# A fused attention and two-layer MLP kernel: the low-part subtraction of a weight tile moved ahead of the next tile's sign step, and the first tiles' conversion rearranged

## The chip, the cores and the metric

The kernel runs on one core of a Trainium2 chip. The metric is the device time of one execution in microseconds (us); lower is better. A profile of one execution gives the time of every instruction on the engines: TensorE (PE in the rows, PEld for its weight loads), VectorE (DVE), ScalarE (ACT), GpSimd (POOL), and SyncE (SP), which issues most DMA transfers.

## The reference

Three stages follow each other. Attention runs in chunks of 64 positions; its output, as a 2304 x 512 matrix x, goes through an MLP with a SiLU, and that result through a gated MLP.

```python
scores = scale * np.matmul(q_c, k_c.transpose(0, 1, 2, 4, 3))   # chunks of 64, 32 heads in all
attn = softmax(scores)
x = np.matmul(attn, v_c)                # as 2304 x 512
h = x @ w_in                            # 512 x 2048
y = (h / (1 + np.exp(-h))) @ w_out      # 2048 x 512
out = ((y @ w_a) * (y @ w_b)) @ w_out2  # 512 x 1536 twice, 1536 x 512
```

The weights arrive as 64-bit floating-point numbers. The kernel turns them into 32-bit ones itself, and splits each into a high part and a low part, since every product is made as three matmuls (high x high, high x low, low x high).

## The kernel before, in words

**Blocks and steps.** The 2304 tokens are 18 tiles of 128. Block 0 is tiles 0 to 3, the side block (`SIDE`) is tiles 4 and 5, and three more blocks of four tiles follow. A step k of the first MLP takes one block and one m of 16 slices of 128 of its hidden width. `front_a` makes the hidden slice (12 matmuls of 512 columns, line L370) and its SiLU on ScalarE: `g` at L399 and its high part `ghi` at L400; `finish` subtracts on VectorE to get the low part `glo` (L396). `back_a` multiplies by the slice of w_out into four accumulating banks (L418). During block 0's 16 steps the side block's fronts and backs, 256 columns wide, go along. In these steps the order on TensorE is: front(k+1), side back(k), side front(k+1), back(k).

**Conversion of a weight tile.** The 32 tiles of w_in and w_out, two for each m, are converted while block 0 runs. A tile passes these functions:

- `fetch`: SyncE loads it into one of three buffers `raws` (L130).
- `scaled`: ScalarE copies the upper words with a scale (L147).
- `magnitude`: two VectorE instructions (L155, L158).
- `begin`: two VectorE instructions that set the sign and the low bits (L174, L178); with the last one the raw buffer is free for the third fetch after it.
- `upper`: ScalarE copies the rounded high part into the tile `wA` (L196).
- `lower`: VectorE subtracts it from the value, which gives the low part (L203). It reads what `upper` wrote, so it waits for it.

`weights` is one call of this pipeline: it fetches a tile, and takes three earlier tiles a stage further. `prep_a` calls it twice in a step, after the SiLU of front(k+1) and after that of side front(k+1). Within a call the order on ScalarE is `upper`, `scaled`; on VectorE it is `magnitude`, `begin`, `lower`. `magnitude` and `begin` work on a later tile than `lower` does. Each engine takes its instructions in the order in which the code issues them (`tc.manual_schedule()`).

**The beginning.** Attention of tiles 0 to 5, the first conversions and the first front and back are written out by hand, as a list of calls: `S(i)` makes scores, `Tr(i, bank)` the transposes (L312) and `rest["P", i]()` their copy out by ScalarE (L316); `V(i, bank)` makes the output of the attention (64x64 matmuls, L335), `rest["X", i]()` its high part on ScalarE (L347), and `rest["L", i]()` its low part on VectorE (L351). `busy(n)` issues n matmuls on a tile of zeros (L705), whose result nobody reads; each shows as two records. They go to the PSUM bank with the tag "sA". The PSUM pool holds one buffer for each tag, so a new tile in bank "sA" waits for the last read of the tile that was in it. `V(4, "sA")` uses this bank too.

The part of the hand-written list around the change, before:

```python
V(4, "sA")
rest["X", 4]()
pend[0], silu = front_a(main[0], 0, "mm", gpool, True)
upper()
Tr(5, "at")
rest["L", 4]()
lower()
silu()
rest["P", 5]()
scaled()
busy(2)
V(5, "mm")
finish(pend, 0)
```

`magnitude`, `begin`, `busy(2)` and `back(0)` follow, then the high and low parts of tile 5, two calls of `prep_a`, and `side_front(0)`. The tile called the third below is the w_in slice of m = 1; it is the one whose `scaled`, `magnitude` and `begin` stand here.

Of the kernel before, what the change touches and what calls it, by code (L numbers as in the profile page):

```python
# [22 lines left out]
def chunk_attention_silu_mlp_gated_mlp(  # L23
# [79 lines left out]
    def bank(tag, shape):  # L103
        return psum.tile(shape, F32, tag=tag, name="ps_" + tag)

    def slot(name, dt=F32R):
        return big.tile([P, 4 * DM], dt, tag="b", name=name)
# [19 lines left out]
    def fetch(src, dest):  # L127
        raw = raws[:, turn[0] % RAWS]
        turn[0] += 1
        nc.sync.dma_start(out=raw, in_=src)  # L130
        fetched.append((dest, raw))

    def leave(n=0):

        while len(leaving) > n:
            dst, src = leaving.pop(0)
            nc.sync.dma_start(out=dst, in_=src)

    def words(raw):
        w32 = raw.bitcast(U32).rearrange("p (f t) -> p f t", t=2)  # L140
        return w32[:, :, 0], w32[:, :, 1]

    def scaled():

        dest, raw = fetched.pop(0)
        w = spool.tile([P, DM], F32, tag="tmp", name="w", bufs=3)
        nc.scalar.activation(w, words(raw)[1].bitcast(F32), AF.Copy, scale=2.0**111)  # L147
        opened.append((dest, raw, w))

    def magnitude():  # L150

        if not opened:
            return
        w = opened[0][2]
        nc.vector.tensor_scalar(  # L155
            out=w, in0=w, scalar1=2.0**-126, scalar2=2.0**-97, op0=ALU.mult, op1=ALU.mult
        )
        nc.vector.tensor_scalar(  # L158
            out=w.bitcast(U32),
            in0=w.bitcast(U32),  # L160
            scalar1=3,
            scalar2=0x7FFFFFFF,
            op0=ALU.logical_shift_left,
            op1=ALU.bitwise_and,
        )

    def begin():

        if not opened:
            return  # L170
        dest, raw, w = opened.pop(0)
        low, high = words(raw)
        wu = w.bitcast(U32)
        nc.vector.scalar_tensor_tensor(  # L174
            out=wu, in0=high, scalar=0x80000000, in1=wu,
            op0=ALU.bitwise_and, op1=ALU.bitwise_or,
        )
        nc.vector.scalar_tensor_tensor(  # L178
            out=wu, in0=low, scalar=29, in1=wu,
            op0=ALU.logical_shift_right, op1=ALU.bitwise_or,  # L180
        )
        if dest[0] == "f":
            wf[dest[1:]] = d = dram.tile([P, DM], F32, name=f"wf{dest[1]}{dest[2]}")
            leaving.append((d, w))
        else:
            stage_1.append((dest, w))

    def upper():
        if not stage_1:
            return  # L190
        dest, w = stage_1.pop()
        _, m, j = dest
        if m not in slots_a:
            slots_a[m] = slot("wA").rearrange("p (j n) -> p j n", j=4)
        hl = slots_a[m][:, 2 * j:2 * j + 2]
        nc.scalar.activation(hl[:, 0], w, AF.Copy)  # L196
        stage_2.append((dest, hl, w))

    def lower():
        if not stage_2:  # L200
            return
        dest, hl, w = stage_2.pop()
        nc.vector.tensor_tensor(out=hl[:, 1], in0=w, in1=hl[:, 0].bitcast(F32), op=ALU.subtract)  # L203
        wA.setdefault(dest[1], {})[dest[2]] = hl[:, 0], hl[:, 1]

    def weights(src, dest):

        leave()
        fetch(src, dest)
        upper()  # L210
        magnitude()
        begin()
        lower()
        scaled()


# [91 lines left out]
    def att_transpose(i, ptag, where, later=False):  # L308
        s = soft.pop(i).rearrange("p h g k -> p h (g k)")
        ps = bank(ptag, [P, KT, P])  # L310
        for hp in range(KT):
            nc.tensor.transpose(ps[:, hp, :], s[:, hp, :], ident)  # L312
        prob[i] = att_tile(where, "pt", i).rearrange("p (h n) -> p h n", h=KT)

        def evacuate():
            nc.scalar.activation(prob[i], ps, AF.Copy)  # L316

        if later:
            return evacuate
        evacuate()  # L320

    def att_values(i, ptags, x, o, later=False, beside=None):
        w = P // len(ptags)
        if beside is None:
            banks = [bank(t, [P, KT, w]) for t in ptags]
        else:
            banks = [t[:, 1 - r] for r, t in enumerate(soft[beside])]
        va = vs.pop(i).rearrange("p (a h d) -> p a h d", a=2, h=KT)
        half = [slice(0, 64), slice(64, 128)]
        for hp in range(KT):  # L330
            for a in range(2):
                for r in range(2):

                    ps, part, n = (banks[0], r, half[a]) if len(banks) == 1 else (banks[r], a, half[0])
                    nc.tensor.matmul(  # L335
                        ps[half[part], hp, n],
                        lhsT=va[half[r], a, hp, :],
                        rhs=prob[i][half[r], hp, half[a]],
                        start=True,
                        stop=True,  # L340
                    )
        parts = [[a[:, :, o + w * j:o + w * j + w] for a in x] for j in range(len(banks))]
        del prob[i]

        def upper():
            for ps, (hi, _) in zip(banks, parts):
                nc.scalar.activation(hi, ps, AF.Copy)  # L347

        def lower():
            for ps, (hi, lo) in zip(banks, parts):  # L350
                nc.vector.tensor_tensor(out=lo, in0=ps, in1=hi.bitcast(F32), op=ALU.subtract)  # L351

        if later:
            return upper, lower
        upper()
        lower()
# [21 lines left out]
    def front_a(b, m, ptag, pool, later=False):  # L378
        n = width(b)
        ps = bank(ptag, [P, n])  # L380
        product(ps, wA[m][0], x_t[b])
        ghi = pool.tile([P, n], F32R, tag="ghi", name="ghi")
        glo = pool.tile([P, n], F32R, tag="glo", name="glo")
        if b == SIDE:
            g = side.tile([P, n], F32, tag="g", name="g")
        elif "g" in late:
            g = late["g"].tile([P, n], F32, tag="g", name="g", bufs=2)
        elif "b" in late:
            g = spool.tile([P, n], F32, tag="tmp", name="g", bufs=3)
        else:  # L390
            if "g1" not in late:
                late["g1"] = late["att"].tile([P, DM], F32, tag="at", name="g")
            g = late["g1"]

        def finish():
            nc.vector.tensor_tensor(out=glo, in0=g, in1=ghi.bitcast(F32), op=ALU.subtract)  # L396

        def silu():
            nc.scalar.activation(g, ps, AF.Silu)  # L399
            nc.scalar.activation(ghi, ps, AF.Silu)  # L400

        if later:
            return (ghi, glo, finish), silu
        silu()
        return ghi, glo, finish
# [239 lines left out]
    def next_a():  # L645
        m, j = units_a[done[0]]
        done[0] += 1
        return (w_in, w_out)[j][m], ("a", m, j)
# [33 lines left out]
    with tc.manual_schedule():  # L682
# [18 lines left out]
        def busy(n):  # L701

            ps = bank("sA", [P, P])
            for _ in range(n):
                nc.tensor.matmul(ps, lhsT=zero, rhs=zero, start=True, stop=True)  # L705

        def half(i):
            if blocks[0][1] > i:
                return x_t[0], i * P
            return x_t[SIDE], (i - blocks[0][1]) * P  # L710
# [9 lines left out]
        def v_in(*tiles):  # L720
            for i in tiles:
                load_v(i, W, nc.sync)
# [12 lines left out]
        qk_in(5)  # L735
        v_in(4)
        v_in(5)


        side_bank = {-1: "at", 0: "at", 1: "at"}  # L740

# [45 lines left out]
        def back(k):  # L787
            b, m = steps[k]
            back_a(b, m, pend.pop(k))
# [9 lines left out]
        def finish(g, k):  # L799
            if k in g:  # L800
                g[k][2]()
# [3 lines left out]
        rest = {}  # L805
# [4 lines left out]
        def Tr(i, tag):  # L810
            rest["P", i] = att_transpose(i, tag, W, later=True)

        def V(i, tag):
            rest["X", i], rest["L", i] = att_values(i, (tag,), *half(i), later=True)
# [35 lines left out]
        rest["X", 1]()  # L850
        att_max(4, W, True)
        begin()
        fetch(*next_a())
        Tr(3, "sA")
        rest["P", 3]()
        rest["L", 1]()
# [22 lines left out]
        rest["X", 4]()  # L879
        pend[0], silu = front_a(main[0], 0, "mm", gpool, True)  # L880
        upper()
        Tr(5, "at")
        rest["L", 4]()
        lower()
        silu()
        rest["P", 5]()
        scaled()
        busy(2)
        V(5, "mm")
        finish(pend, 0)  # L890
        magnitude()
        begin()
        busy(2)
        back(0)
        rest["X", 5]()
# [430 lines left out]
```

## Time and profile before

| | us |
|---|---|
| median of 3 runs | 863.20 (862.88 to 863.54) |
| the profiled execution | 862.69 |
| its span, first to last instruction | 860.9 |
| TensorE busy in the span | 846.5 (98%) |
| VectorE busy | 566.7 (66%) |
| ScalarE busy | 398.5 (46%) |

The span is 1.8 us shorter than the time of the same execution. The mean granted clock of TensorE was 0.999 of full speed. Busy shares are averages over stages with different limits; of the 14.4 us in which TensorE was idle, 3.6 lie behind its last matmul and most of the rest in the first 46 us.

### The profile page before, as it was taken

To read this page: it belongs to the slowest core of one execution; us is meant where nothing else is said; L and a number is where in the kernel's file an instruction comes from. 1 tells how busy PE (TensorE), PEld (TensorE's weight loads), DVE (VectorE), ACT (ScalarE), POOL (GpSimd) and SP (SyncE) were. 2 spreads that over 40 slices of the span, in tenths; PEclk is the share of its full clock that TensorE was granted. 3 is DMA by queue.
4 is the path that set the end of the run, shared out by engine and by line. 5 is a ranking of instruction groups with operands and counts; after the bars stand their busy time and mean duration, and the time that the engine had idled before them with its cause. 6 is when DMAs were issued, how large, how long until landed. Compare 5 with 4: busy or idle time off the path is not lost.

```text
span 860.9 us, 14124 instructions
## 1 busy us (share of the span) xinstructions
PE 846.5 (98%) x5474; PEld 769.5 (89%) x5474; DVE 566.7 (66%) x1029; ACT 398.5 (46%) x769; POOL 50.2 (6%) x91
## 2 busy tenths in 40 slices
PE   7999999999999999999999999999999999999998
PEld 7788888888888888888889999999999999999998
DVE  6886877855567755757865997584454594454563
ACT  5645546535454455434545554463333373333252
POOL 0000000010010100023201110000000000000000
PEclk9999999999999999999999999999999999999999
DMA  8354353337455654467799887878666888666761
GB/s 294 100 174 132 123 161 121 100 118 238 147 174 172 217 165 169 152 226 269 265 343 372 314 296 309 306 297 294 256 249 254 306 313 265 245 252 252 288 226 56
DMA packets 54034, 193.85 MB, mean 225 GB/s; under 512 B 5904, under 2 KB 13584, under 8 KB 45520
## 3 DMA queue, kind: packets, MB, share of 16 engines
q1 hardware_dynamic: 46752, 169.76, 55.5%
q0 software_dynamic: 6928, 22.81, 8.0%
q8 instruction: 43, 0.70, 0.3%
q10 hardware_dynamic: 288, 0.39, 0.1%
q14 instruction: 23, 0.19, 0.1%
HBM read 141.03 MB, written 51.90 MB: 224 GB/s over the span
## 4 chain that ended last, share of the span: by engine, by line
PE 86%; issue 5%; ACT 3%; DMA 3%; DVE 3%; POOL 0%; POOLq 0%; ACTq 0%; DVEq 0%
PE ps_acc L972 19%; PE ps_acc L418 19%; PE ps_mm L370 15%; PE ps_sA L370 7%; PE ps_at L972 5%; PE ps_sA L972 5%; PE ps_sB L972 4%; PE ps_mm L972 4%; DMA raws<-wf 2%; PE ps_sA L418 1%; PE ps_sB L418 1%; PE ps_at L370 1%; PE ps_at L253 1%; PE ps_at L335 1%; PE ps_sA L705 1%
## 5 line engine op out<-in xcount | busy, mean ns | idle before, releaser
L972 PE MATMUL ps_acc<-xo,ring 128*128 128x384 f32 x868 | 168.2, 334 | 0.6 <-DVE gq L1047 0.6
L418 PE MATMUL ps_acc<-ghi,wA 128*128 128x512 f32 x512 | 159.2, 392 | 0.0
L972 PEld LDWEIGHTS ps_acc<-xo,ring 128*128 128x128 f32 x868 | 152.1, 188 | 1.1 <-DVE gq L1047 1.1
L418 PEld LDWEIGHTS ps_acc<-ghi,wA 128*128 128x128 f32 x512 | 94.2, 188 | 19.1
L370 PE MATMUL ps_mm<-xhi,wA 128*128 128x512 f32 (+1 forms) x400 | 101.3, 375 | 3.2 <-ACT wA L196 3.2
L418 PE MATMUL ps_acc<-glo,wA 128*128 128x512 f32 x256 | 99.9, 390 | 0.0
L370 PEld LDWEIGHTS ps_mm<-xhi,wA 128*128 128x128 f32 x400 | 70.2, 188 | 17.3 <-ACT wA L196 5.1
L399 ACT ACTIVATE g<-ps_mm 128x512 f32<-128x512 f32 (+1 forms) x50 | 28.0, 559 | 102.5 <-PE ps_mm L370 96.3
L396 DVE TENSOR_TENSOR glo<-g,ghi 128x512 fp32r<-128x512 f32 x80 | 50.7, 633 | 27.2 <-ACT ghi L400 27.0
L418 PEld LDWEIGHTS ps_acc<-glo,wA 128*128 128x128 f32 x256 | 48.1, 188 | 10.2
L1107 DVE TENSOR_TENSOR u<-gq,u 128x384 fp32r<-128x384 f32 x84 | 44.5, 553 | 17.4 <-ACT u L1106 16.9
L1106 ACT ACTIVATE u<-gq 128x384 fp32r<-128x384 f32 x84 | 40.6, 516 | 30.5 <-DVE gq L1047 28.6
L972 PE MATMUL ps_acc<-u,ring 128*128 128x384 f32 x272 | 53.6, 337 | 0.3
L147 ACT ACTIVATE w<-raws 128x512 f32<-128x512 f32 x68 | 45.5, 670 | 16.6 <-DMA raws<-w_b 8.8
L370 PE MATMUL ps_mm<-xlo,wA 128*128 128x512 f32 (+1 forms) x200 | 49.9, 371 | 0.6 <-DVE xlo L351 0.6
L370 PE MATMUL ps_sA<-xhi,wA 128*128 128x512 f32 x184 | 49.6, 391 | 0.0
L972 PEld LDWEIGHTS ps_acc<-u,ring 128*128 128x128 f32 x272 | 47.6, 188 | 1.3 <-ACT gq L981 0.9
L178 DVE SCALAR_TENSOR_TENSOR w<-raws,w 128x512 uint32<-128x512 uint32 x68 | 47.1, 692 | 2.3
L174 DVE SCALAR_TENSOR_TENSOR w<-raws,w 128x512 uint32<-128x512 uint32 x68 | 47.1, 692 | 2.3
L972 PE MATMUL ps_at<-xo,ring 128*128 128x384 f32 x231 | 47.8, 334 | 0.0
L972 PE MATMUL ps_sB<-xo,ring 128*128 128x384 f32 x220 | 44.9, 334 | 0.0
L972 PE MATMUL ps_sA<-xo,ring 128*128 128x384 f32 x213 | 44.4, 335 | 0.1
(183 smaller groups left out, 1413.5 us busy)
## 6 DMA issues: line engine op xcount, KB each, us to landing
ring<-w SPq DMA_DIRECT2D x30, 1024.0 KB, 7.3
ring<-wg SPq DMA_DIRECT2D x24, 1024.0 KB, 5.1
ring<-wg SPq DMA_DIRECT2D x24, 768.0 KB, 6.3
wg<-ring SPq DMA_DIRECT2D x12, 1024.0 KB, 6.6
wf<-w SPq DMA_DIRECT2D x36, 256.0 KB, 2.2
wg<-ring SPq DMA_DIRECT2D x12, 768.0 KB, 6.5
raws<-w_in SPq DMA_DIRECT2D x16, 512.0 KB, 3.5
raws<-w_out SPq DMA_DIRECT2D x16, 512.0 KB, 3.5
```

The source lines that it names most:

```text
L147: nc.scalar.activation(w, words(raw)[1].bitcast(F32), AF.Copy, scale=2.0**111)
L174: nc.vector.scalar_tensor_tensor(out=wu, in0=high, scalar=0x80000000, in1=wu, op0=ALU.bitwise_and, op1=ALU.bitwise_or,)
L178: nc.vector.scalar_tensor_tensor(out=wu, in0=low, scalar=29, in1=wu, op0=ALU.logical_shift_right, op1=ALU.bitwise_or,)
L253: nc.tensor.matmul(soft[i][j % len(soft[i])][n, j, hp, :], lhsT=q[r, hp, n], rhs=k[r, hp, n], start=True, stop=True,)
L335: nc.tensor.matmul(ps[half[part], hp, n], lhsT=va[half[r], a, hp, :], rhs=prob[i][half[r], hp, half[a]], start=True, stop=True,)
L370: nc.tensor.matmul(ps, lhsT=a[:, kk * P:(kk + 1) * P], rhs=b[:, kk, :], start=(j == 0 and kk == 0), stop=(j == 2 and kk == KT - 1),)
L396: nc.vector.tensor_tensor(out=glo, in0=g, in1=ghi.bitcast(F32), op=ALU.subtract)
L399: nc.scalar.activation(g, ps, AF.Silu)
L418: nc.tensor.matmul(acc_t[b][j], lhsT=a[:, j * P:(j + 1) * P], rhs=g, start=(m == 0 and i == 0 and (b != SIDE or j % 2 == 0)), stop=(m == M ...
L972: nc.tensor.matmul(ps, lhsT=a, rhs=b, start=first and i == 0, stop=last and i == 2, skip_group_check=True,)
L1106: nc.scalar.activation(hi, src, AF.Copy)
L1107: nc.vector.tensor_tensor(out=lo, in0=src, in1=hi.bitcast(F32), op=ALU.subtract)
```

## The change

There are two parts. In `weights`, `lower` is issued ahead of `begin`. In the hand-written beginning, the third fetch is issued right after the attention's loads, `scaled` of the third tile goes ahead of `Tr(5)`, `magnitude` ahead of `finish`, and `rest["L", 4]()`, the low part of tile 4 of x, goes from before the SiLU to behind `begin`.

```diff
@@ weights
         upper()
         magnitude()
+        lower()
         begin()
-        lower()
         scaled()
@@ beginning
         v_in(5)
-
+        fetch(*next_a())
...
         begin()
-        fetch(*next_a())
         Tr(3, "sA")
...
         upper()
+        scaled()
         Tr(5, "at")
-        rest["L", 4]()
         lower()
         silu()
         rest["P", 5]()
-        scaled()
         busy(2)
         V(5, "mm")
+        magnitude()
         finish(pend, 0)
-        magnitude()
         begin()
+        rest["L", 4]()
         busy(2)
         back(0)
```

VectorE at the beginning, from the end of tile 5's softmax (L303) to the low part of tile 5 of x (the second L351). In the kernel before:

```order
L303 TENSOR_TENSOR start<-start,rs 128x2x4x64
L351 TENSOR_TENSOR xlo<-ps_sA,xhi 128x4x128
L203 TENSOR_TENSOR wA<-w,wA 128x512
L396 TENSOR_TENSOR glo<-g,ghi 128x512
L155 TENSOR_SCALAR w<-w 128x512
L158 TENSOR_SCALAR w<-w 128x512
L174 SCALAR_TENSOR_TENSOR w<-raws,w 128x512
L178 SCALAR_TENSOR_TENSOR w<-raws,w 128x512
L351 TENSOR_TENSOR xlo<-ps_mm,xhi 128x4x128
```

The same place in the changed kernel:

```order
L303 TENSOR_TENSOR start<-start,rs 128x2x4x64
L203 TENSOR_TENSOR wA<-w,wA 128x512
L155 TENSOR_SCALAR w<-w 128x512
L158 TENSOR_SCALAR w<-w 128x512
L396 TENSOR_TENSOR glo<-g,ghi 128x512
L174 SCALAR_TENSOR_TENSOR w<-raws,w 128x512
L178 SCALAR_TENSOR_TENSOR w<-raws,w 128x512
L351 TENSOR_TENSOR xlo<-ps_sA,xhi 128x4x128
L351 TENSOR_TENSOR xlo<-ps_mm,xhi 128x4x128
```

The read of bank "sA" (L351 on ps_sA) went from the first place behind the softmax to the seventh, behind the subtraction for `glo` and both instructions of `begin`. TensorE's own order is the same in both kernels: the transposes of tile 5, two busy matmuls into ps_sA, the 64x64 matmuls of V(5), two more busy matmuls, back(0).

VectorE in the first call of step 0, from `glo` of side front(0) to `glo` of front(1). In the kernel before:

```order
L396 TENSOR_TENSOR glo<-g,ghi 128x256
L155 TENSOR_SCALAR w<-w 128x512
L158 TENSOR_SCALAR w<-w 128x512
L174 SCALAR_TENSOR_TENSOR w<-raws,w 128x512
L178 SCALAR_TENSOR_TENSOR w<-raws,w 128x512
L203 TENSOR_TENSOR wA<-w,wA 128x512
L396 TENSOR_TENSOR glo<-g,ghi 128x512
```

In the changed kernel:

```order
L396 TENSOR_TENSOR glo<-g,ghi 128x256
L155 TENSOR_SCALAR w<-w 128x512
L158 TENSOR_SCALAR w<-w 128x512
L203 TENSOR_TENSOR wA<-w,wA 128x512
L174 SCALAR_TENSOR_TENSOR w<-raws,w 128x512
L178 SCALAR_TENSOR_TENSOR w<-raws,w 128x512
L396 TENSOR_TENSOR glo<-g,ghi 128x512
```

The subtraction of the earlier tile, L203, now stands ahead of L174 and L178 of the next one, and so in each later call. On SyncE the order of the transfers is the same in both kernels; the third fetch stood directly behind the attention's loads already.

## Rows read from the trace of the kernel before

**Rows 1.** The page: engines' busy time, and the chain that ended last by engine.
```profile
PE 846.5 (98%) x5474; PEld 769.5 (89%) x5474; DVE 566.7 (66%) x1029; ACT 398.5 (46%) x769; POOL 50.2 (6%) x91
...
PE 86%; issue 5%; ACT 3%; DMA 3%; DVE 3%; POOL 0%; POOLq 0%; ACTq 0%; DVEq 0%
```

**Rows 2.** Waits of TensorE: us in total, times, longest.
```profile
PE ps_mm L370 <- ACT wA L196: 3.2, 5, 1.3
```

**Rows 3.** Timeline of TensorE: start, us, instruction, count, [idle before, its releaser].
```profile
30.96 0.60 PE L312 MATMUL ps_at<-ident,start 128*128 128x128 f32 x4
31.40 0.69 PE L705 MATMUL ps_sA<-start 128*128 128x128 f32 x4
32.79 1.15 PE L335 MATMUL ps_mm<-start 64*64 64x64 f32 x32 [0.70 <-ACT start L316]
33.87 0.71 PE L705 MATMUL ps_sA<-start 128*128 128x128 f32 x4
34.33 0.71 PE L418 MATMUL ps_acc<-ghi,wA 128*128 128x512 f32 x2
```

**Rows 4.** Timeline of VectorE, 30 to 36 us.
```profile
30.02 0.69 DVE L303 TENSOR_TENSOR start<-start,rs 128x512 f32<-128x512 f32 x1
30.64 0.68 DVE L351 TENSOR_TENSOR xlo<-ps_sA,xhi 128x512 fp32r<-128x512 f32 x1
31.24 0.68 DVE L203 TENSOR_TENSOR wA<-w,wA 128x512 fp32r<-128x512 f32 x1
32.28 0.69 DVE L396 TENSOR_TENSOR glo<-g,ghi 128x512 fp32r<-128x512 f32 x1 [0.36 <-ACT ghi L400]
33.32 0.43 DVE L155 TENSOR_SCALAR w<-w 128x512 f32<-128x512 f32 x1 [0.35 <-ACT w L147]
...
34.25 0.69 DVE L174 SCALAR_TENSOR_TENSOR w<-raws,w 128x512 uint32<-128x512 uint32 x1
34.97 0.69 DVE L178 SCALAR_TENSOR_TENSOR w<-raws,w 128x512 uint32<-128x512 uint32 x1
35.58 0.68 DVE L351 TENSOR_TENSOR xlo<-ps_mm,xhi 128x512 fp32r<-128x512 f32 x1
```

**Rows 5.** Timeline of ScalarE, 27 to 34 us.
```profile
27.89 0.63 ACT L196 ACTIVATE wA<-w 128x512 fp32r<-128x512 f32 x1
...
31.16 0.60 ACT L399 ACTIVATE g<-ps_mm 128x512 f32<-128x512 f32 x1 [1.34 <-PE ps_mm L370]
...
32.61 0.68 ACT L147 ACTIVATE w<-raws 128x512 f32<-128x512 f32 x1
```

**Rows 6.** Timelines of VectorE, ScalarE and TensorE at step 0.
```profile
43.27 0.69 DVE L203 TENSOR_TENSOR wA<-w,wA 128x512 fp32r<-128x512 f32 x1 [1.09 <-ACT wA L196]
...
44.99 0.63 ACT L196 ACTIVATE wA<-w 128x512 fp32r<-128x512 f32 x1
...
45.68 1.20 PE L370 MATMUL ps_mm<-xhi,wA 128*128 128x512 f32 x4 [1.27 <-ACT wA L196]
```

**Rows 7.** Timelines of VectorE and ScalarE in a later step, with attention of tile 6.
```profile
67.86 0.69 DVE L203 TENSOR_TENSOR wA<-w,wA 128x512 fp32r<-128x512 f32 x1 [2.40 <-ACT wA L196]
...
69.19 0.69 DVE L272 TENSOR_TENSOR s<-ps_at,mx 128x512 f32<-128x512 f32 x1
...
71.87 0.63 ACT L283 ACTIVATE s<-s 128x512 f32<-128x512 f32 x1
```

**Rows 8.** Timeline of TensorE: its first matmuls, its longest early pause, its last matmuls.
```profile
1.09 5.37 PE L705 MATMUL ps_sA<-start 128*128 128x128 f32 x24 [1.09 <-DVE start L699]
...
10.04 0.81 PE L253 MATMUL ps_acc<-start 64*64 64x64 f32 x32 [1.62 <-DMA start<-kt]
...
856.12 1.21 PE L972 MATMUL ps_sA<-u,ring 128*128 128x384 f32 x6
```

**Rows 9.** Stretches at the end: us, busy by engine, granted clock, DMA share, GB/s.
```profile
859.00:859.50 0.50, 0.00 (x0) 0.00 (x0) 0.00 (x0) 0.00 (x0) 0.00 (x0) 1.00 0.57 203
859.50:860.00 0.50, 0.00 (x0) 0.00 (x0) 0.00 (x0) 0.00 (x0) 0.00 (x0) 0.54 0.00 0
```

## The prediction, made before the result

> **What bounds the kernel now.** I read the page first: TensorE is busy for 846.5 of 860.9 us, and 86% of the chain that ended last is on it [rows 1]. So a change counts where it makes TensorE wait longer or shorter, and nowhere else. The waits of TensorE come next. Those for converted weight tiles (matmul L370 for ScalarE's copy L196) are five, 3.2 us in all, the longest 1.3 [rows 2]; this is all that a better order of the conversion could win. None of the waits names the subtraction L203. Then the timelines of the beginning, engine by engine, since there the change rewrites the order [rows 3, 4, 5], and two places in the steps behind it [rows 6, 7].
>
> The reader is to see one thing in the beginning. TensorE issues two busy matmuls into bank ps_sA at 31.40 [rows 3], and VectorE's read L351 of that bank, the low part of tile 4, started at 30.64 and took 0.68, so it ended at 31.32 [rows 4]. The busy matmuls came 0.08 us behind it. The view of waits shows no idle time there, because the transposes before (30.96, for 0.60) filled it. The dependence is there all the same: one buffer for each tag, and a new tile in it must wait for the last read of the old one.
>
> **The change, part by part.**
>
> *The read of ps_sA.* In the changed order L351 stands behind L203, L155, L158, L396, L174 and L178. TensorE's order is not changed, so the busy matmuls still wait for L351, and V(5) and back(0) stand behind them. With the slots of VectorE (from one start to the next) I place the new row:
> - L203 takes the slot that L351 had, at 30.64, and the next one starts 0.60 later, at 31.24.
> - `magnitude` (L155 and L158) takes 34.25 - 33.32 = 0.93, to 32.17. Its input is there, see below.
> - L396 still waits for `ghi`, which comes from ScalarE behind front(0); so it starts at 32.28 as before. Its slot is 0.60, as that of L351: 32.88.
> - L174 takes 34.97 - 34.25 = 0.72, to 33.60; L178 takes 35.58 - 34.97 = 0.61, to 34.21 [rows 4].
> - L351 runs from 34.21 to 34.89, instead of to 31.32.
>
> With the same 0.08 the busy matmuls start at 34.97. Four records of them hold TensorE for 34.33 - 33.87 = 0.46, so V(5) starts at 35.43 instead of 32.79, 2.64 later [rows 3]. The 0.70 of idle time that stood ahead of V(5), for ScalarE's copy L316, is used up in this. The rest of the beginning hangs on V(5) in order (busy, back(0) at 34.33, the side block), so it is all late by **2.64**. TensorE has no slack to give it back: what it waits for later, it waits for relative to its own products.
>
> *The steps: L203 ahead of L174.* L203 waits for `upper`, which ScalarE does behind the SiLU of the same call. So far this wait cost nothing, as L174 and L178 ran ahead of it. Now they wait too, and the next tile's `upper` waits for them. At step 0 this reaches TensorE. L203 starts at 43.27, when its copy is done [rows 6]. In the new order L174 starts 0.60 later at 43.87, L178 at 44.59, and that ends at 45.28. ScalarE's next L196 started at 44.99, and TensorE's front waits for exactly that one (1.27, at 45.68) [rows 6]. It is late by 45.28 - 44.99 = **0.29**.
>
> In the later steps the delay is covered. The hardest is a step with attention, where L203 waited 2.40 us and started at 67.86 [rows 7]. L174 and L178 now push the attention's subtraction L272 back by 0.72 + 0.61 = 1.33: it ends at 69.19 + 0.69 + 1.33 = 71.21, and the exponential that reads it starts at 71.87 [rows 7], behind a table load that does not wait for it. So 0.66 is left. If that cover were gone, each of the four such steps could lose up to 1.33, 5.3 in all; I take nothing, and keep it for the upper end. There is no gain either: TensorE waits for L196, not for L203.
>
> *Moved earlier.* `scaled` (0.68) now stands behind L196, which ends at 28.52; ScalarE was idle for 1.34 ahead of the SiLU at 31.16, waiting for TensorE [rows 5]. It fits in, and `magnitude` finds it done at 31.24. The fetch keeps its place on SyncE. The tile's `begin` ends at 34.3 instead of 35.66, but its copy L196 stands on ScalarE behind the high part of tile 5, which now follows the late V(5). So of this head start nothing is left, and nothing waited for it. All these I cost at nothing; without their cover `scaled` would cost its 0.68.
>
> *The clock.* TensorE's pause grows: its transposes end at 31.56, the next matmul comes at 34.97, so 3.4 us. A pause of 1.62 us, ahead of 10.04, left the granted clock at 1.00 [rows 8]. At the end of the kernel the last matmuls ended at 856.12 + 1.21 = 857.33, and the clock fell to half (0.5, that is 1.2 of 2.4 GHz) in the stretch from 859.50 on, 2.2 us after them [rows 8, 9]. The new pause is longer than that. So I expect the clock to fall in it or right behind it. What a fall costs no row shows in the middle of the kernel. The bound below is nothing: the clock stays or comes back at once. For the bound above I take the start: busy matmuls ran there for 5.37 us at 5.37 / 24 = 0.22 us a record, against 0.46 / 4 = 0.115 later [rows 3, 8], so half speed for some 5.2 us; half of that is 2.6 lost. I take **1.8**, nearer to the upper end, since the row of the start is the only one with a price.
>
> The Trainium skill (TensorE: Matmul & The Clock Gate, "Why this matters for your kernels") warns of such idle gaps between bursts of matmuls, after which the clock is back at half until the engine has been busy again. By this rule the sum has the clock's term; without it it ends at 2.9. The end of this trace agrees with it, at 2.2 us.
>
> **The sum.** 2.64 + 0.29 = 2.93 of waiting, and 1.8 for the clock: 4.7. Against the profiled execution's own time, 860.9 + 1.8 outside the span = 862.7, this gives 867.4. The median of the runs is 0.5 above that execution, so 863.2 + 4.7 = 867.9, and I say **868.0 us**.
>
> **Rivals.**
> - *The clock stays up.* Then 863.2 + 2.93 = 866.1. For it: no pause inside the kernel was followed by a lower clock. Against: none was half as long.
> - *The delay is given back.* If VectorE and ScalarE, being ahead of a late TensorE, had the tiles ready, the 3.2 us of waits for L196 would vanish: 863.2 + 2.93 - 3.2 = 862.9, no change. Against: the copies stand on ScalarE behind the SiLU of TensorE's own product, and so move along with it.
> - *Faster.* The place is the same wait, L370 for L196. If the busy matmuls did not hang on L351 and the earlier `lower` let the copies come sooner, all 3.2 us could go: 860.0. It decides in its favour only if the busy matmuls stay at about 31.4, and the wait at 45.68 shrinks. The 0.08 between L351's end and the busy matmuls speaks against it.
> - *The steps lose as well.* If the 0.66 ahead of the exponential is not there (a later start of L203, a late transfer), up to 5.3 more: 868 to 873, I take 871.
>
> The Trainium skill (PSUM — Partial Sum Buffer, "Engine vs sequencer instructions") says that matmuls start and complete in program order. By this V(5) cannot pass the waiting busy matmuls; if it could, it would start at 32.79 and the 2.64 would not be. The matmuls' starts in the trace agree: they stand in program order, 31.40, 32.79, 33.87, 34.33 [rows 3].
>
> **How the numbers follow.** The clock falls: 0.50. It stays: 0.35. The steps lose as well: 0.07. Given back: 0.05. Faster: 0.03. A change under 0.2% (1.7 us) can't be told from none here. Both likely cases are slower by more than that, so slower 0.92, same 0.05, faster 0.03. For the range: if the clock stays, 866.1, and 0.5 less if VectorE's slots are a little shorter; if it falls, up to 866.1 + 2.6 = 868.7, and an engine that runs slow right behind its pause may lose 1 more. That makes 865.6 to 869.8, which leaves out the last three cases and little more.
>
> **What would show it.** The busy matmuls L705 start near 35.0, with some 3.4 us idle ahead of them, put down to VectorE's L351 on ps_sA; V(5) near 35.4. The wait ahead of step 0's second front, 1.27 before, is near 1.6. The four waits of about 0.5 us later stay. The granted clock is below 1.00 for some us from about 34 on; if it is 1.00 throughout, the term of 1.8 is wrong. If the busy matmuls start at 31.4, the prediction is wrong altogether.

## The result, and the profile after

The changed kernel took 867.32 us (median of 6 runs, 866.87 to 869.22), the kernel before on the same chip 862.90. The ratio is 1.0054, with a 95% interval from 1.0041 to 1.0067: slower by 3.5 to 5.8 us. The span of the profiled execution grew from 860.9 to 865.9 us.

The new wait stands in the view of TensorE's waits of the changed kernel (us in total, times, longest):

```profile
PE ps_mm L370 <- ACT wA L196: 3.5, 5, 1.6
PE ps_sA L705 <- DVE xlo L351: 3.4, 1, 3.4
```

The first line answers to [rows 2]; the second had no counterpart. The timeline of TensorE at the beginning, for [rows 3]:

```profile
31.44 0.60 PE L312 MATMUL ps_at<-ident,start 128*128 128x128 f32 x4
35.44 0.71 PE L705 MATMUL ps_sA<-start 128*128 128x128 f32 x4 [3.40 <-DVE xlo L351]
36.08 1.46 PE L335 MATMUL ps_mm<-start 64*64 64x64 f32 x32
37.47 1.22 PE L705 MATMUL ps_sA<-start 128*128 128x128 f32 x4
38.34 1.20 PE L418 MATMUL ps_acc<-ghi,wA 128*128 128x512 f32 x2
...
43.47 1.08 PE L370 MATMUL ps_mm<-xhi,wA 128*128 128x512 f32 x4
```

The timeline of VectorE there, for [rows 4], shows what the busy matmuls (L705) waited for. The read of ps_sA starts at 34.70, behind six other instructions, and ends at 35.38:

```profile
31.10 0.69 DVE L203 TENSOR_TENSOR wA<-w,wA 128x512 fp32r<-128x512 f32 x1
31.70 0.42 DVE L155 TENSOR_SCALAR w<-w 128x512 f32<-128x512 f32 x1
...
32.76 0.69 DVE L396 TENSOR_TENSOR glo<-g,ghi 128x512 fp32r<-128x512 f32 x1 [0.17 <-ACT ghi L400]
33.37 0.69 DVE L174 SCALAR_TENSOR_TENSOR w<-raws,w 128x512 uint32<-128x512 uint32 x1
34.09 0.69 DVE L178 SCALAR_TENSOR_TENSOR w<-raws,w 128x512 uint32<-128x512 uint32 x1
34.70 0.68 DVE L351 TENSOR_TENSOR xlo<-ps_sA,xhi 128x512 fp32r<-128x512 f32 x1
```

Behind the pause the granted clock fell to half. In these stretches of the changed kernel the first number after the POOL column is the granted clock:

```profile
36.00:37.00 1.00, 1.00 (x28) 0.92 (x28) 0.00 (x0) 0.00 (x0) 0.00 (x0) 0.86 0.72 242
37.00:38.00 1.00, 1.00 (x13) 0.88 (x11) 0.00 (x0) 0.42 (x1) 0.00 (x0) 0.50 0.59 238
...
39.00:40.00 1.00, 1.00 (x4) 0.81 (x3) 0.97 (x3) 0.85 (x2) 0.00 (x0) 0.50 0.00 0
40.00:41.00 1.00, 1.00 (x5) 0.78 (x5) 0.97 (x2) 0.00 (x0) 0.00 (x0) 0.93 0.00 0
```

From the shares 0.86 and 0.93 it was at half from about 36.7 to 40.1 us. At step 0, for [rows 6], the timelines of VectorE, ScalarE and TensorE:

```profile
48.09 0.69 DVE L203 TENSOR_TENSOR wA<-w,wA 128x512 fp32r<-128x512 f32 x1 [2.51 <-ACT wA L196]
...
49.42 0.69 DVE L178 SCALAR_TENSOR_TENSOR w<-raws,w 128x512 uint32<-128x512 uint32 x1
...
50.15 0.63 ACT L196 ACTIVATE wA<-w 128x512 fp32r<-128x512 f32 x1 [0.21 <-DVE w L178]
...
50.83 1.20 PE L370 MATMUL ps_mm<-xhi,wA 128*128 128x512 f32 x4 [1.59 <-ACT wA L196]
```

ScalarE's copy L196 now waits for `begin` (L178), and TensorE's wait for that copy is 1.59 us instead of 1.27. In the step with attention, for [rows 7], the subtraction L272 moved close to the exponential, but not past it:

```profile
75.68 0.69 DVE L272 TENSOR_TENSOR s<-ps_at,mx 128x512 f32<-128x512 f32 x1
...
77.04 0.64 ACT L283 ACTIVATE s<-s 128x512 f32<-128x512 f32 x1
```

It ends at 76.37, and 0.67 is left. The four later waits of TensorE for L196 stayed at 0.47 to 0.48.

**Where the 5.0 us of the span went.** From the transposes of tile 5 to V(5) there are 36.08 - 31.44 = 4.64 us, before 32.79 - 30.96 = 1.83 [rows 3]: 2.81 more. From V(5) to the first front of the steps there are 43.47 - 36.08 = 7.39 us; in the kernel before that front stood here in TensorE's timeline:

```profile
38.61 1.09 PE L370 MATMUL ps_mm<-xhi,wA 128*128 128x512 f32 x4
```

That is 38.61 - 32.79 = 5.82, so 1.57 more, with the same instructions in both. Step 0 adds 1.59 - 1.27 = 0.32. The transposes themselves came 0.48 later (31.44 against 30.96). The wait for a transfer ahead of the first scores was 0.4 us longer in this execution, but that had been made up by the transposes of tile 2 (17.44 against 17.54). The delay came up behind them, in V(1), where TensorE paused and the profile shows no instruction that it waited for ("issue"):

```profile
18.61 0.97 PE L335 MATMUL ps_acc<-start 64*64 64x64 f32 x26 [0.28 <-issue]
```

The run low_alone, which has neither the early fetch nor the early `scaled`, shows the same 0.28 at this place, and filled, which has both, does not. So the 0.48 belongs to this execution and is no part of the change's price. Together 5.18; some 0.2 is won back where waits near the end were shorter.

### The profile page after: what moved, and what is told of

Its sections match the earlier page's. It is cut to its first block, busy times and chain, and to the rows that moved or that the text cites. A ratio compares the mean times of both kernels' runs of the same rounds, so it can differ in the third digit from the quotient of the medians.

```text
span 865.9 us, 14124 instructions
## 1 busy us (share of the span) xinstructions
PE 848.4 (98%) x5474; PEld 770.9 (89%) x5474; DVE 564.3 (65%) x1029; ACT 399.0 (46%) x769; POOL 50.0 (6%) x91
## 4 chain that ended last, share of the span: by engine, by line
PE 84%; issue 6%; DVE 4%; ACT 3%; DMA 2%; POOL 0%; ACTq 0%; POOLq 0%; DVEq 0%
PE ps_acc L418 19%; PE ps_acc L971 19%; PE ps_mm L370 14%; PE ps_sA L370 7%; PE ps_at L971 5%; PE ps_sA L971 5%; PE ps_sB L971 4%; PE ps_mm L971 4%; DMA raws<-wf 2%; PE ps_sA L418 1%; PE ps_at L370 1%; PE ps_sB L418 1%; PE ps_at L335 1%; PE ps_sA L705 1%; PE ps_at L253 1%
## 5 line engine op out<-in xcount | busy, mean ns | idle before, releaser
L178 DVE SCALAR_TENSOR_TENSOR w<-raws,w 128x512 uint32<-128x512 uint32 x68 | 47.1, 692 | 2.3
L174 DVE SCALAR_TENSOR_TENSOR w<-raws,w 128x512 uint32<-128x512 uint32 x68 | 46.9, 689 | 1.3
```

The source lines that it names most:

```text
L174: nc.vector.scalar_tensor_tensor(out=wu, in0=high, scalar=0x80000000, in1=wu, op0=ALU.bitwise_and, op1=ALU.bitwise_or,)
L178: nc.vector.scalar_tensor_tensor(out=wu, in0=low, scalar=29, in1=wu, op0=ALU.logical_shift_right, op1=ALU.bitwise_or,)
```

## The experiments

Each run was timed beside the kernel before on the same chip; the ratios are to that.

**low_back.** The changed kernel with the one line back in its place:

```diff
         Tr(5, "at")
+        rest["L", 4]()
         lower()
...
         begin()
-        rest["L", 4]()
         busy(2)
```

> The changed kernel with the low part of tile 4 of x back in its old place, ahead of the third tile's magnitude; all else as changed. If the read of bank sA is the cause: the busy matmuls start within 0.2 us of the end of that read, near 31.5 to 32, the granted clock stays at 1.00, and 2.64 us of waiting and some 1.7 us of low clock are gone; only the 0.3 us at step 0 is left, 863.0 to 863.5 us against 862.9. If the conversion's order in the steps is the cause (the earlier subtraction holding up the next tile), the time stays at 867.

863.11 us, ratio 1.0004 (0.9995 to 1.0013). Timelines of TensorE and VectorE:

```profile
31.35 0.69 PE L705 MATMUL ps_sA<-start 128*128 128x128 f32 x4
32.74 1.15 PE L335 MATMUL ps_mm<-start 64*64 64x64 f32 x32 [0.70 <-ACT start L316]
...
30.58 0.68 DVE L351 TENSOR_TENSOR xlo<-ps_sA,xhi 128x512 fp32r<-128x512 f32 x1
```

The read ends at 31.26 and the busy matmuls start at 31.35. The granted clock stays at 1.00 here (it was at half much earlier in this execution, see the last section). All of the loss that the times can show hung on this line; of the rest of the change only the 0.3 us at step 0 shows, in the waits.

**low_alone.** The kernel before with that line moved, alone:

```diff
         Tr(5, "at")
-        rest["L", 4]()
         lower()
...
         begin()
+        rest["L", 4]()
         busy(2)
         back(0)
```

> The kernel before with that one line moved behind begin, and nothing else. There begin ends at 35.66, later than in the changed kernel, so the read ends near 36.3 and the busy matmuls start near 36.4 instead of 31.4; V(5) is late by 4.0 us, and a pause of 4.8 us brings the clock down: 1.7 us more. The theory gives 868.6 us. If the line alone costs nothing and it takes the rest of the change, 863.

869.36 us, ratio 1.0073 (1.0060 to 1.0086). In its timeline of TensorE:

```profile
37.01 0.97 PE L705 MATMUL ps_sA<-start 128*128 128x128 f32 x4 [4.75 <-DVE xlo L351]
```

The line is enough by itself, and the price follows how late the read is: the pause is 4.75 us here, where `begin` comes later. From the transposes to the first front the trace shows 5.7 us more than before, and 4.4 in the changed kernel (2.81 + 1.57). So the earlier `scaled` and `magnitude` of the change softened the loss. By the times the loss is 0.19% more than that of the changed kernel, but the two intervals meet. The clock was at half from 37.3 to 40.7 us in the profiled execution, whose mean granted clock is 0.998; three of the other four have 0.994, so they were at half for longer, and no trace shows where.

**other_bank.** The changed kernel with the first two busy matmuls in another bank:

```diff
-        busy(2)
+        busy(2, "sB")
         V(5, "mm")
```

> The changed kernel, with the first two busy matmuls (zeros, read by nobody) sent to bank sB, whose last read is long over by then, instead of bank sA. If the wait is for the bank: no wait, clock at 1.00, 863.0 to 863.5 us, though the low part of tile 4 stays where the change put it. If that late low part is itself needed by something on TensorE's path (the side block reads it), the time stays above 865.

865.34 us, ratio 1.0020 (1.0011 to 1.0030). By the time alone this is the second case of the expectation, above 865. The timeline of TensorE shows something else:

```profile
32.68 0.60 PE L312 MATMUL ps_at<-ident,start 128*128 128x128 f32 x4
33.12 0.61 PE L705 MATMUL ps_sB<-start 128*128 128x128 f32 x4
34.51 1.15 PE L335 MATMUL ps_mm<-start 64*64 64x64 f32 x32 [0.78 <-ACT start L316]
36.68 0.71 PE L705 MATMUL ps_sA<-start 128*128 128x128 f32 x4 [1.02 <-DVE xlo L351]
```

The first pair no longer waits, but the second pair, behind V(5), goes to ps_sA too, and waits 1.02 us for the same read. I had overlooked it.

That is only a part of the time. In the profiled execution (865.8 us, span 864.0) the transposes of tile 5 stood at 32.68, 1.72 later than in the kernel before, after transfer waits of 3.7 us among the first scores (1.6 before) and half the clock from 10.8 to 17.6 us. Behind them V(5) to the first front takes 6.91 us, 1.09 more than before, and step 0 costs 0.32. So the place itself is worth 1.4 us. The nine executions lie between 863.59 and 865.86, and their median is not the price of the second pair.

**both_other.** The same with both pairs in bank sB:

```diff
-        busy(2)
+        busy(2, "sB")
         back(0)
```

> The changed kernel with the first and the second pair of busy matmuls of this place in bank sB; in the run other_bank the second pair still waited 1.0 us for the read of bank sA. If the bank is all there is to it, no busy matmul waits for that read, V(5) to back(0) stand as in the kernel before, and the time is 0.3 us above it (step 0): ratio 1.000 to 1.001. If the late low part costs in another way, the ratio stays at 1.002.

862.93 us, ratio 1.0006 (0.9997 to 1.0015). TensorE:

```profile
31.47 0.61 PE L705 MATMUL ps_sB<-start 128*128 128x128 f32 x4
...
33.94 0.71 PE L705 MATMUL ps_sB<-start 128*128 128x128 f32 x4
```

Nothing waits for the read of bank sA any more, though that read stays where the change put it. V(5) stands at 32.86 (32.79 before). It was the shared bank that made the late read dear; the late low part of tile 4 holds up nothing else on TensorE.

**filled.** The changed kernel with the pause filled with work:

```diff
+        busy(14, "sB")
         busy(2)
         V(5, "mm")
```

> The changed kernel with 14 more busy matmuls, into bank sB, ahead of the two that wait: they fill 3.2 us of the pause, so the wait is still there but TensorE is at work during it. If the clock's term is a thing of its own: the granted clock stays at 1.00 and the time is 1.7 us below that of the changed kernel, near 865.6. If the low clock cost nothing, or had another cause than the pause, 867.3.

865.88 us, ratio 1.0036 (1.0023 to 1.0048). TensorE, and stretches in which the changed kernel was at half the clock:

```profile
31.22 3.29 PE L705 MATMUL ps_sB<-start 128*128 128x128 f32 x28
34.77 0.71 PE L705 MATMUL ps_sA<-start 128*128 128x128 f32 x4 [0.27 <-DVE xlo L351]
35.41 1.15 PE L335 MATMUL ps_mm<-start 64*64 64x64 f32 x32
...
41.22 1.09 PE L370 MATMUL ps_mm<-xhi,wA 128*128 128x512 f32 x4
...
37.00:38.00 1.00, 1.00 (x7) 0.83 (x7) 0.76 (x2) 1.00 (x3) 0.00 (x0) 1.00 0.05 21
38.00:39.00 1.00, 1.00 (x6) 0.84 (x5) 0.97 (x3) 0.86 (x2) 0.00 (x0) 1.00 0.00 0
39.00:40.00 1.00, 1.00 (x7) 0.84 (x6) 0.96 (x2) 0.00 (x0) 0.00 (x0) 1.00 0.00 0
```

V(5) starts 4.63 us behind the transposes, as late as in the changed kernel, but the clock stays at 1.00 here, and from V(5) to the first front there are 41.22 - 35.41 = 5.81 us, as before the change. So the clock's part is the 1.57 us of the accounting above, read from one profiled execution of each kernel. By the times it is (1.0054 - 1.0036) x 863 = 1.6, though their intervals meet.

**calls_alone.** The kernel before with the order in `weights` changed, alone:

```diff
         magnitude()
+        lower()
         begin()
-        lower()
         scaled()
```

> The kernel before with the subtraction ahead of begin in weights, and nothing of the beginning changed. The theory: 0.3 us at step 0, where the wait of the front matmuls for the copy L196 grows from 1.27 to about 1.6, and the four later waits stay at 0.48: 863.2 us, not to be told from 862.9 by the time, but by the waits. If the steps lose as well (attention's exponential late), the four waits grow to 1.1 and the time is 865 or more.

862.86 us, ratio 1.0003 (0.9994 to 1.0011). TensorE at step 0 and in the first of the four later steps:

```profile
45.93 1.20 PE L370 MATMUL ps_mm<-xhi,wA 128*128 128x512 f32 x4 [1.59 <-ACT wA L196]
...
73.30 1.21 PE L370 MATMUL ps_mm<-xhi,wA 128*128 128x512 f32 x4 [0.48 <-ACT wA L196]
```

The wait at step 0 grew to 1.59, as forecast, and the later ones did not. The time can't show 0.3 us; the waits do.

**early_copy.** Not a part of the change. The kernel before, with the second copy of five steps ahead of the side front's SiLU:

```diff
+            if k in (0, 3, 6, 9, 12):
+                upper()
             side_front(k + 1)
```

> Not a part of the change: the kernel before, with the second copy L196 of steps 0, 3, 6, 9 and 12 issued on ScalarE ahead of the side front's SiLU and not behind it. If the five waits of TensorE hang on ScalarE's order, as the prediction read them, they go, all 3.2 us, and the time is 859.7 to 860.5 us. If they hang on VectorE's begin of that tile, the waits stay or move and the time stays near 862.9.

859.48 us, ratio 0.9966 (0.9953 to 0.9978). The four later waits are gone. Step 0, on ScalarE, VectorE and TensorE:

```profile
43.96 0.62 ACT L196 ACTIVATE wA<-w 128x512 fp32r<-128x512 f32 x1
44.76 0.39 ACT L399 ACTIVATE g<-ps_at 128x256 f32<-128x256 f32 x1 [0.19 <-PE ps_at L370]
...
46.98 0.68 DVE L203 TENSOR_TENSOR wA<-w,wA 128x512 fp32r<-128x512 f32 x1
...
47.72 1.20 PE L370 MATMUL ps_mm<-xhi,wA 128*128 128x512 f32 x4 [0.99 <-DVE wA L203]
```

The second call's own `upper()` then finds nothing left to do. The copy fits into ScalarE's idle time ahead of the side front's SiLU. The wait for L196 is gone at step 0 too, but one of 0.99 us for the subtraction L203 took its place: the first eight matmuls of the front, which use the high part of the weights, now run without a wait, and the last four, which use the low part, come before L203 is done.

The view of waits would let one expect 3.2 - 0.99 = 2.2 us; the span shrank from 860.9 to 857.9, by 3.0. The four later waits, 0.48 each in that view, were worth more than they show: from one such front to the next there were 102.22 - 73.07 = 29.15 us in the kernel before, and there are 100.98 - 72.61 = 28.37 here, 0.78 less. Part of it is that the front itself ran slower behind the wait: from its first matmul to its ninth 1.95 us, here 1.81.

**early_both.** There the change's own idea has a use: the subtraction ahead of `begin`, but only in the calls whose copy is early; the `lower()` behind `begin` then finds nothing left to do.

```diff
         magnitude()
+        if low_first:           # second call of steps 0, 3, 6, 9, 12
+            lower()
         begin()
         lower()
```

> The run early_copy with the subtraction ahead of begin as well, but only in the second call of steps 0, 3, 6, 9 and 12, where its copy is done early. In early_copy a wait of 0.99 us for that subtraction came up at step 0; it should go: 1.0 us below early_copy, near 858.5. If the subtraction's place is worth nothing even there, or begin's delay costs as much, the time equals that of early_copy.

858.56 us, ratio 0.9954 (0.9941 to 0.9966). On VectorE at step 0:

```profile
45.70 0.68 DVE L203 TENSOR_TENSOR wA<-w,wA 128x512 fp32r<-128x512 f32 x1
```

L203 starts at 45.70, directly behind `magnitude`, and no wait of TensorE for L196 or L203 is left. This version beats both kernels.

**early_copy_again.** The run for comparison:

> The run early_copy once more, beside early_both on the same chip: 859.5 us, and a ratio to the kernel before of 0.996 to 0.997.

859.38 us, ratio 0.9965 (0.9952 to 0.9977). So early_both is 0.8 us below it, near the 0.99 of the wait; the intervals of the two ratios meet, and it is the waits that show the step.

## Why the prediction was right

*The read of ps_sA.* Right in mechanism, place and size. The busy matmuls were to start at 34.97; they started at 35.44 in an execution whose transposes came 0.48 late. Forecast 2.64, measured 2.81: I took 0.46 us for the four records of busy matmuls, and ahead of V(5) they took 36.08 - 35.44 = 0.64. In filled they took 0.64 too, behind an idle time of only 0.27 and at full clock, so the pair ahead of back(0) was the wrong row to take the slot from. low_back, low_alone and both_other tie the loss to this line and to the shared bank.

*The steps.* Forecast 0.29, measured 0.32, by the path named: L203 waits for its copy, `begin` waits for L203, the next copy for `begin`. The cover of the exponential was to be 0.66 and was 0.67. calls_alone shows both without the rest. So the rival "the steps lose as well" did not happen.

*The clock.* Forecast 1.8, measured 1.57 by the trace. The clock did fall, but 1.3 us after work had begun again, not in the pause, and it was back after 3.4 us. filled shows that it was the pause that brought it down. The rival "the clock stays" fails by this term alone; the waits by themselves are what filled measured, 1.0036.

That the term came out so near was partly luck. It was a choice between 0 and 2.6. The upper bound was read from the length of the busy matmuls at the start, where the stretches show a granted clock of 1.00; the clock's record in the trace begins only at 6.2 us, so those rows neither confirm half the clock there nor deny it. The argument by the length of the pause held here, but not as a rule (last section). The 1 us more that the range allowed to an engine that runs slow behind its pause came from no row, and no run shows it. And the 1.57 is from one execution: the slowest of the six, 869.22 us, has a mean clock of 0.994 against 0.998 in the profiled one, so it was at half for longer, and no trace of it is kept.

*The other rivals.* "Given back" did not happen: the five waits for L196 grew from 3.2 to 3.5 us, since these copies stand behind the SiLU of TensorE's own products. "Faster" named the right place, that same wait, and early_copy wins there; but what it takes first is the copy's place on ScalarE; the subtraction's place on VectorE pays only behind that, in early_both. The bound of 3.2 us for a better order of the conversion was too low: early_both is 3.9 us below the kernel before (858.56 against 862.50), since a wait can cost more than the idle time that it shows.

*The sum.* 868.0 was forecast, 867.32 measured. By the trace the terms were 2.81, 0.32 and 1.57, 4.70 together, against 4.73: the first came out 0.17 above its forecast and the last 0.23 below, and they nearly cancel. The medians lie 4.42 apart, and the forecast had started from 863.2 where the kernel before then took 862.90.

## What to carry to other kernels

Work that nobody reads still obeys its buffer: before a read of a shared bank is moved back, look for who next writes that bank, filler matmuls first of all. A wait that shows as 0 in the list of waits, because an instruction ahead just covers it, is a dependence all the same, and here 0.08 us between an end and a start gave it away. Where an engine with no slack waits for a copy, ask which instructions stand ahead of the copy on its own engine, rather than what comes after it.

## What the runs showed of the hardware that was not expected

The clock can fall after much shorter pauses than the change made, and the length of the pause alone does not decide it. In low_back TensorE paused 1.80 us for a transfer early on, and the clock was at half 1.1 us after work had begun again. TensorE's row, then stretches of that run:

```profile
10.24 0.81 PE L253 MATMUL ps_acc<-start 64*64 64x64 f32 x32 [1.80 <-DMA start<-kt]
...
10.00:11.00 1.00, 0.76 (x33) 0.72 (x33) 0.90 (x4) 1.00 (x9) 0.00 (x0) 1.00 1.07 412
11.00:12.00 1.00, 1.00 (x9) 1.00 (x7) 1.00 (x3) 0.33 (x3) 0.00 (x0) 0.68 1.08 422
12.00:13.00 1.00, 1.00 (x6) 0.78 (x5) 0.90 (x5) 0.00 (x0) 0.00 (x0) 0.50 0.99 381
```

In the kernel before a pause of 1.62 us at this place left the clock up [rows 8]; so did one of 2.00 us in the changed kernel (in filled, 1.99 us there did not):

```profile
10.44 0.81 PE L253 MATMUL ps_acc<-start 64*64 64x64 f32 x32 [2.00 <-DMA start<-kt]
...
11.00:12.00 1.00, 1.00 (x23) 0.86 (x13) 0.90 (x4) 1.00 (x8) 0.00 (x0) 1.00 1.09 432
12.00:13.00 1.00, 0.61 (x6) 0.42 (x4) 1.00 (x3) 0.03 (x1) 0.00 (x0) 1.00 0.99 395
```

Seven of the eleven traces show such an early fall; those of the kernel before, the changed kernel, low_alone and calls_alone do not. What decides between them these runs do not show.

The span of low_back's execution was 860.9 us all the same, as in the kernel before: in attention TensorE has waits for VectorE (0.88 us ahead of tile 0's transposes in the kernel before, none here), and the slower matmuls ran in that time. So a fall of the clock costs what TensorE's own chain is worth in that stretch: 1.57 us behind the pause of the change, nothing that shows in low_back. It need not be free early on: in other_bank it was at half for 6.8 us from 10.8 on; the scores there began 1.22 us later than in the kernel before, after longer transfers, and the transposes of tile 2, behind the half clock, 1.71 us later.
